# Turning gate rows on TensorE instead of by DMA, one result bank, and a new written-out order, in a fused dynamic-convolution and top-1 expert kernel

## The chip, the cores and the metric

One core of a Trainium2 chip runs the whole kernel. The metric is the device time of one execution in microseconds; lower is better. Engines are named as the profile names them: PE (TensorE matmuls), PEld (its weight loads), DVE (VectorE), ACT (ScalarE), POOL (GpSimd) and SP (SyncE, which here only issues transfers).

## The reference

There are 8 x 3584 = 28,672 tokens of 192 channels. The first half is a causal convolution whose 7 weights per token and head are a softmax; the second half sends every token to the one of 8 experts that its gate prefers.

```
w = softmax(weight_gen, axis=-1)                       # (8, 3584, 8 heads, 7 taps)
attn[b,s,h,:] = sum_k w[b,s,h,k] * x_pad[b, s+k, h, :]  # 24 channels a head
x = attn.reshape(28672, 192)
logits = x @ w_gate + modality_bias[modality_id]        # 8 experts
e = argmax(logits); p = softmax(logits)[e]
out[n] = p[n] * (relu(x[n] @ w1[e]) @ w2[e])            # 192 -> 1024 -> 192
```

## The kernel before

The tokens go through in 16 units of 1,792 tokens (128 partitions x 14 tokens), and each unit passes these steps; the name in brackets is the token of the step in the order string, followed by the unit's number.

- Load of weights, inputs and modality (LU, lines 366 to 379, on SP's queue).
- Softmax (A, X, SM, SN, B, and from unit 6 on BN: line 563 writes the normalised weights of half a unit into a PSUM bank instead of over the loaded ones).
- The 7 taps. In early units products (M, L581) are summed by PE (S, L593); later DVE multiplies (PQ, L569) and adds (PA, PM, L614, L618), and some sums are made by POOL's accumulating transfers (DA, L609).
- A scale for the unit from two ACT passes over the input, whose output is thrown away into a scratch tile "junk" (SA, L502).
- Rows: the sum split into a high and a low half-precision part in a row buffer (H on ACT, L624; L on DVE, L632 and L633).
- Gate: the rows of 128 tokens have to be turned so that channels lie on partitions. Units 0 to 4 do it on PE: six transposes into the single PSUM bank "gt" (T, L642), a copy to "xg" by ACT (E, L646). Units 5 to 15 do it by 14 transposing transfers on SP's queue each (XT, L653), from the row buffer straight into "xg", which has three buffers of two tokens each. Then PE multiplies (G, L666, into "lg").
- Routing (RA, RB and others on DVE), a table of the next expert batches (TB on DVE, read by SP), and 14 scatters of the rows to DRAM by POOL (SC, L738).

The experts' half works on 138 batches ("pages" in the code) of 128 or 256 rows of one expert: 51 of 128 and 87 of 256. A batch is fetched by a transposing transfer (PL, L960, into "xT", four buffers) and its expert's weights, if they changed, by another (PW, L979, 1.8 MB). PE computes the first layer in groups of 1,024 PSUM columns (HM, L1002, 225 groups, two buffers of two banks), ACT takes relu to "hi" (HA, L1014), DVE the remainder "lo" (HL, L1018), PE the second layer (OM, 24 matmuls at L1029 to L1031, 225 groups, into "g2", two banks), ACT scales the result into "ot" (OA, L1036) and POOL scatters it (OS, L1041).

PSUM has eight banks: four for the first layer, two for the second, and one each for "gt" and "lg". The softmax weights of BN share the bank of "gt", which in those units has no transposes.

Nothing is scheduled at run time: every engine takes its instructions in the order of the string ORDER, one token a step, and the instructions wait on semaphores for what they read and overwrite. The string interleaves the batches of earlier units with the convolution of later ones.

Of the kernel before, what the change touches and what calls it, by code (L numbers as in the profile page):

```python
# [63 lines left out]
T.0.3 S.1.0.2 wlo.3.0 E.0.3 wld.6 wpf.2 wpf.3 wlo.3.1 G.0.3 wsq.5.0 T.0.4 E.0.4 wst.2 M.1.0.3 T.0.5 wst.3 wsq.5.1 G.0.4
M.1.0.4 S.1.0.3 E.0.5 M.1.0.5 XB.2 G.0.5 T.0.6 M.1.0.6 S.1.0.4 E.0.6 A.2 G.0.6 wtr.5 S.1.0.5 RA.0.0 X.2 wmx.5 wts.2
RA.0.1 BP.2 RA.0.2 wsc.5 M.1.1.0 XM.2 S.1.0.6 wts.3 RA.0.3 wsq.6.0 wdg.5 M.1.1.1 RX.0 RA.0.4 SA.2.0 wbc.5 M.1.1.2
S.1.1.0 RA.0.5 SM.2 wsf.5 H.1.0 RA.0.6 S.1.1.1 M.1.1.3 whi.4.0 wld.7 RB.0.0 L.1.0 wsq.6.1 RR.0 S.1.1.2 whi.4.1 RB.0.1
wlo.4.0 SE.0 SN.2 wpf.4 T.1.0 SA.2.1 RB.0.2 S.1.1.3 wlo.4.1 whi.5.0 RB.0.3 wst.4 M.1.1.4 wts.4 E.1.0 RB.0.4 S.1.1.4
# [1073 lines left out]
```

## Time and profile before

| | |
|---|---|
| three timed runs, median (lowest to highest) | 1264.75 us (1251.67 to 1268.13) |
| the profiled execution, its own time | 1245.94 us |
| its span, first to last instruction | 1244.2 us |
| mean granted TensorE clock | 0.955 of full |
| PE busy | 1118.4 us (90%) |
| DVE busy | 969.5 us (78%) |
| ACT busy | 581.3 us (47%) |
| POOL busy | 651.7 us (52%) |

The span falls into three stages. Up to about 150 us no expert batch has begun. From there to about 1008 us, where the last gate matmul ends, PE works on batches while DVE works on the convolution. After that only batches are left. A busy share of PE is modelled for pipelined matmuls, so the count of instructions in a stretch of time tells more than its busy time.

### The profile page before, as it was taken

The page shows a single profiled execution, that of the slowest core. Times are in us where ns is not written, and L with a number is a line of the kernel's source. Part 1 is how long each engine was busy: PE and PEld are TensorE (multiplying, and loading weights), DVE is VectorE, ACT ScalarE, POOL GpSimd, SP SyncE. Part 2 cuts the span into 40 slices and gives each one's busy share as a digit, 9 for nine tenths or more (in the row PEclk, how much of TensorE's full clock was granted, in tenths as well). Part 3 has the DMA queues.
Part 4 walks back from the last instruction along what each step waited for, and adds up shares of the span by engine and source line. Part 5 has one row for each costly group of instructions (what it writes and reads, how often), then busy time and mean ns, then how long its engine had stood idle before and what let it go on. Part 6 is the DMA issues. An engine that isn't in the chain of part 4 may idle for free.

```text
span 1244.2 us, 31134 instructions
## 1 busy us (share of the span) xinstructions
PE 1118.4 (90%) x12304; PEld 1007.8 (81%) x12304; DVE 969.5 (78%) x1197; ACT 581.3 (47%) x1025; POOL 651.7 (52%) x561
## 2 busy tenths in 40 slices
PE   6698897599799799999799969997979999999997
PEld 3344497599689799999699959997969999999997
DVE  7799999699789799999599969999788852322231
ACT  3987274374445345464345434544333433333432
POOL 5007778488745566666337663657365465222222
PEclk9799998899989899999799989999999999999999
DMA  9988779987888778889989897969698644142243
GB/s 312 311 309 328 239 161 277 136 178 174 208 192 172 147 192 167 186 173 242 177 175 167 187 222 142 223 128 181 132 188 178 119 119 97 43 136 72 50 134 118
DMA packets 241110, 220.55 MB, mean 177 GB/s; under 512 B 198593, under 2 KB 215229, under 8 KB 235586
## 3 DMA queue, kind: packets, MB, share of 16 engines
q1 hardware_dynamic: 211776, 137.75, 45.4%
q0 software_dynamic: 29184, 80.77, 31.6%
q8 instruction: 98, 1.61, 0.6%
q14 instruction: 52, 0.42, 0.1%
HBM read 305.03 MB, written 60.05 MB: 293 GB/s over the span
## 4 chain that ended last, share of the span: by engine, by line
PE 58%; DMA 17%; issue 9%; DVE 6%; SPq 3%; POOL 3%; ACT 2%; POOLq 0%; DVEq 0%; ACTq 0%
PE g L1002 30%; PE g L1029 9%; PE g L1031 9%; PE g L1030 9%; DMA xg<-rows 6%; DMA xT<-rows_scratch 5%; POOL out_dram L1041 2%; DMA rows_scratch<-rows,idx 2%; DVE prod L581 2%; DMA wc<-in_moe_w_dram 2%; SPq L653 1%; DMA w<-weights_scratch 1%; PE lg L666 1%; PE acc L593 1%; DMA xt<-in_x_dram 1%
## 5 line engine op out<-in xcount | busy, mean ns | idle before, releaser
L1002 PE MATMUL g<-xT,w 128*128 128x256 f16 (+1 forms) x5520 | 548.9, 258 | 15.5 <-DMA xT<-rows_scratch 14.4
L1002 PEld LDWEIGHTS <-w 128*128 128x128 f16 x5520 | 464.8, 100 | 58.4 <-issue 11.0
L1031 PE MATMUL g<-w,lo 128*128 128x192 f16 x1800 | 446.8, 248 | 14.9 <-DVE lo L1018 13.9
L1041 POOL DMA_INDIRECT out_dram<-ot,meta x225 | 257.1, 1143 | 366.7 <-ACT ot L1036 311.9
L1029 PE MATMUL g<-w,hi 128*128 128x192 f16 x1800 | 446.5, 248 | 0.0
L1030 PE MATMUL g<-w,hi 128*128 128x192 f16 x1800 | 446.5, 248 | 0.0
L1018 DVE SCALAR_TENSOR_TENSOR lo<-g,hi 128x1024 f16<-128x1024 f32 x225 | 273.3, 1215 | 217.7 <-ACT hi L1014 217.0
L738 POOL DMA_INDIRECT rows_scratch<-rows,idx x224 | 327.3, 1461 | 156.1 <-ACT rows L733 78.6
L1014 ACT ACTIVATE hi<-g 128x1024 f16<-128x1024 f32 x225 | 229.9, 1022 | 349.9 <-PE g L1002 343.2
L1031 PEld LDWEIGHTS <-lo 128*128 128x128 f16 x1800 | 177.7, 99 | 18.9 <-DVE lo L1018 17.4
L1036 ACT ACTIVATE ot<-g,gm 128x192 f32<-128x192 f32 x225 | 94.0, 418 | 188.1 <-PE g L1031 117.3
L1030 PEld LDWEIGHTS <-hi 128*128 128x128 f16 x1800 | 177.7, 99 | 1.9
L1029 PEld LDWEIGHTS <-hi 128*128 128x128 f16 x1800 | 177.6, 99 | 1.9
L614 DVE TENSOR_TENSOR sum<-sum,tmp 128x1344 f32<-128x1344 f32 x78 | 120.3, 1543 | 0.0
L593 PE MATMUL acc<-prod,ident 128*128 128x512 f32 (+1 forms) x240 | 101.7, 573 | 17.9 <-DVE prod L581 17.8
L593 PEld LDWEIGHTS acc<-prod,ident 128*128 128x128 f32 x240 | 46.0, 199 | 64.2 <-issue 54.4
L569 DVE TENSOR_TENSOR tmp<-gt,xt 128x1344 f32<-128x1344 f32 x60 | 92.6, 1543 | 0.0
L609 POOL DMA_DIRECT2D sum<-prod x53 | 51.5, 979 | 49.4 <-DMA sum<-prod 16.2
L666 PE MATMUL lg<-wg,xg 128*128 128x16 f16 x672 | 34.3, 171 | 47.2 <-DMA xg<-rows 45.1
L666 PEld LDWEIGHTS <-xg 128*128 128x128 f16 x672 | 31.6, 98 | 52.3 <-DMA xg<-rows 47.4
L581 DVE TENSOR_TENSOR prod<-xt,wt 128x1344 f32<-128x1344 f32 x41 | 63.0, 1550 | 4.4 <-PE acc L593 4.3
L569 DVE TENSOR_TENSOR prod<-gt,xt 128x1344 f32<-128x1344 f32 x40 | 61.7, 1543 | 0.0
(138 smaller groups left out, 825.4 us busy)
## 6 DMA issues: line engine op xcount, KB each, us to landing
w<-weights_scratch SPq DMA_DIRECT2D x138, 1792.5 KB
sum<-prod POOLq DMA_DIRECT2D x53, 672.0 KB
xt<-in_x_dram SPq DMA_DIRECT2D x15, 1920.0 KB
weights_scratch<-hw SPq DMA_DIRECT2D x8, 1280.5 KB
wt<-in_weight_gen_dram SPq DMA_DIRECT2D x16, 392.0 KB
wc<-in_moe_w_dram SPq DMA_DIRECT2D x8, 768.0 KB
wa<-in_moe_w_dram SPq DMA_DIRECT2D x8, 512.0 KB
weights_scratch<-hw SPq DMA_DIRECT2D x16, 256.0 KB
```

The costliest lines, as they stand in the source:

```text
L569: return nc.vector.tensor_tensor(to.rearrange("p t (h g) -> p t h g", h=H), win, xin, ALU.mult)
L593: nc.tensor.matmul(un[u]["psum", c][:, q], lhsT=ident32, rhs=un[u]["pr", c, k][:, q], start=(k == order[0]), stop=(k == order[-1]))
L614: return nc.vector.tensor_tensor(a, a, un[u]["tmp"], ALU.add)
L738: i = nc.gpsimd.indirect_dma_start(out=rows, out_offset=bass.IndirectOffsetOnAxis(ap=idx[:, j:j + 1], axis=0), in_=ri[:, j, 0:ROW // 2], i ...
L1002: nc.tensor.matmul(o, lhsT=wt[:, w0:w0 + P], rhs=xT[:, xi, :pt], start=(q * pt % 512 == 0 and j == 0), stop=(j == 4), skip_group_check=True)
L1014: return nc.scalar.activation(hi, pg["ps", grp], AF.Relu)
L1018: return nc.vector.scalar_tensor_tensor(lo, live[i]["ps", grp], 0.0, hi, op0=ALU.max, op1=ALU.subtract)
L1029: nc.tensor.matmul(ps, lhsT=hi, rhs=wt[:, w0:w0 + D], start=(f == 0), stop=False)
L1030: nc.tensor.matmul(ps, lhsT=hi, rhs=wt[:, w0 + D:w0 + 2 * D], start=False, stop=False)
L1031: nc.tensor.matmul(ps, lhsT=lo, rhs=wt[:, w0:w0 + D], start=False, stop=(f == NFT - 1))
L1036: nc.scalar.activation(ot, pg["out", t], AF.Copy, scale=pg["gm"][:, t:t + 1])
L1041: w = nc.gpsimd.indirect_dma_start(out=out, out_offset=bass.IndirectOffsetOnAxis(ap=pg["meta"][:, t, 1:2], axis=0), in_=pg["res", t], in_o ...
```

## The change

Five edits:

1. Units 5 to 15 turn their gate rows on PE as units 0 to 4 did: the 88 XT steps (154 transposing transfers) go, 77 T steps and 77 E steps come. G is then done in seven steps of two tokens in these units too, with the same 42 matmuls a unit. "xg" gets four buffers.
2. The second layer's results get one PSUM bank instead of two. The bank that comes free holds the softmax weights, so "gt" is free for transposes.
3. BN, softmax weights in PSUM, begins at unit 4 instead of unit 6.
4. The scratch tile that takes the thrown-away output of the scale passes has one-byte elements instead of two-byte ones.
5. The order string is made anew, as far as the end of the last batches of the middle stage; the tail differs in a few places.

A step that loads a unit's input in pieces (LX) is added too, but no token of the new order uses it.

```
-XG = 3
-PS1 = 2
+XG = 4
+XCUTS = (0, 5, 10, 15, 20)
+PS1, PS2 = 2, 1
...
-HM.37.0 OA.36.1 ... XT.7.3 TB.6.0 PQ.7.1.6 OS.36.0 G.7.1 ...
+T.7.0 OA.35.1 PW.39 HM.37.0 E.7.0 HL.36.1 ... T.7.1 HA.37.0 OM.36.0 ... E.7.1 GM.37 T.7.2 ...
...
-        junk = att.tile([P, half * D], BF16, name="junk", bufs=1)
+        junk = att.tile([P, half * D], U8, name="junk", bufs=1)
...
-            pool["wn"] = psg.tile([P, 512], F32, name="gt")
+            pool["wn"] = (pool["psw"] if PS2 == 1 else psg).tile([P, 512], F32, name="wn" if PS2 == 1 else "gt")
...
-            junk = att.tile([P, (HALO + TU) // 2 * D], BF16, name="junk", bufs=1)
+            junk = att.tile([P, (HALO + TU) // 2 * D], U8, name="junk", bufs=1)
...
-        if fn == "HM" and args == [0, 0]:
+        if (fn == "BN" and PS2 == 1 or name == "HM.0.0") and "ps1" not in pool:
             early_ps.close()
             pool["ps1"] = ctx.enter_context(tc.tile_pool(name="ps1", bufs=PS1, space=PSUM))
-            pool["ps2"] = ctx.enter_context(tc.tile_pool(name="ps2", bufs=2, space=PSUM))
+            pool["ps2"] = ctx.enter_context(tc.tile_pool(name="ps2", bufs=PS2, space=PSUM))
+            if PS2 == 1:
+                pool["psw"] = ctx.enter_context(tc.tile_pool(name="psw", bufs=1, space=PSUM))
```

(The two lines of the order are cut from longer ones.)

What moves on SP's queue is shown at the load of unit 13: "xt" is that load, "xT" and "meta" a batch, "w" an expert's weights, "xg" gate rows of unit 11 being turned, and TENSOR_LOAD reads the table of batches. Before:

```order
L377 DMA xt<-in_x_dram 128x3840
L379 DMA mt<-in_moe_modality_id_dram 128x28
L947 TENSOR_LOAD tb
L960 ISA
L960 DMA_TRANSPOSE xT<-rows_scratch 128x3x256
L962 ISA
L962 DMA meta<-rows_scratch 128x2x2
L653 DMA_TRANSPOSE xg<-rows_73 128x3x128 x2
L979 ISA
L979 DMA w_1076<-weights_scratch 128x3585
```

And now, from the same load on:

```order
L382 DMA xt<-in_x_dram 128x3840
L384 DMA mt<-in_moe_modality_id_dram 128x28
L959 TENSOR_LOAD tb
L972 ISA
L972 DMA_TRANSPOSE xT<-rows_scratch 128x3x256
L974 ISA
L974 DMA meta<-rows_scratch 128x2x2
L991 ISA
L991 DMA w_1115<-weights_scratch 128x3585
L959 TENSOR_LOAD tb
L972 ISA
```

The transposes of gate rows behind the load are gone, and the next batch's transfers follow directly.

What moves on ACT is shown where unit 11's first rows are turned: "hi" and "ot" are the two evictions of a batch, "gm" its scale, "se", "sm" and "rows_72" small steps of the units' softmax and routing. Before:

```order
L730 ACTIVATE se<-se 128x14
L1036 ACTIVATE ot<-g_10615,gm 128x192
L1014 ACTIVATE hi<-g_10653 128x1024
L531 ACTIVATE wt<-wt 128x784
L1036 ACTIVATE ot<-g_10695,gm 128x192
L542 ACTIVATE sm<-sm 128x112
L733 ACTIVATE rows_72<-se,sf 128x14
L1014 ACTIVATE hi<-g_10736 128x1024
```

And now:

```order
L742 ACTIVATE se<-se 128x14
L999 ACTIVATE gm<-meta,w_1114 128x2
L1048 ACTIVATE ot<-g_10752,gm 128x192
L658 ACTIVATE xg<-gt 128x768
L1026 ACTIVATE hi<-g_10791 128x1024
L658 ACTIVATE xg<-gt 128x768
L1048 ACTIVATE ot<-g_10841,gm 128x192
L745 ACTIVATE rows_72<-se,sf 128x14
L658 ACTIVATE xg<-gt 128x768
L1026 ACTIVATE hi<-g_10884 128x1024
```

Three copies of turned rows now stand between the evictions, one about every half batch.

## Rows read from the trace of the kernel before

**Rows 1.** Page, part 4: the chain that ended last, by line.
```profile
PE g L1002 30%; PE g L1029 9%; PE g L1031 9%; PE g L1030 9%; DMA xg<-rows 6%; DMA xT<-rows_scratch 5%; POOL out_dram L1041 2%; DMA rows_scratch<-rows,idx 2%; DVE prod L581 2%; DMA wc<-in_moe_w_dram 2%; SPq L653 1%; DMA w<-weights_scratch 1%; PE lg L666 1%; PE acc L593 1%; DMA xt<-in_x_dram 1%
```

**Rows 2.** Stretches of 40 us: PE, PEld, DVE, ACT, POOL, clock, DMA, GB/s.
```profile
320.00:360.00 40.00, 33.84 (x312) 29.57 (x311) 31.89 (x37) 18.39 (x33) 26.25 (x22) 0.87 0.99 240
...
400.00:440.00 40.00, 32.32 (x337) 29.37 (x335) 30.57 (x42) 16.60 (x30) 22.30 (x19) 0.91 0.74 147
440.00:480.00 40.00, 40.00 (x458) 37.87 (x457) 39.75 (x53) 21.52 (x42) 28.78 (x22) 1.00 0.85 191
...
600.00:640.00 40.00, 35.04 (x328) 31.74 (x329) 33.27 (x34) 12.89 (x21) 15.17 (x14) 0.83 0.91 173
...
720.00:760.00 40.00, 29.84 (x308) 27.07 (x306) 27.93 (x33) 15.31 (x31) 19.60 (x20) 0.87 1.09 201
...
840.00:880.00 40.00, 32.04 (x336) 29.79 (x334) 30.37 (x40) 16.77 (x31) 27.51 (x23) 0.87 0.99 196
...
920.00:960.00 40.00, 31.13 (x318) 28.24 (x317) 28.86 (x32) 11.74 (x19) 23.24 (x20) 0.87 0.89 172
```

**Rows 3.** Waits over the whole span: in total us, times, longest.
```profile
ACT ot L1036 <- PE g L1031: 117.3, 95, 9.2
...
PE lg L666 <- DMA xg<-rows: 45.1, 13, 10.0
ACT rows L624 <- DVE sum L618: 24.1, 10, 11.3
...
PE g L1002 <- DMA xT<-rows_scratch: 14.4, 4, 7.0
...
PE gt L642 <- ACT xg L646: 8.7, 6, 2.7
```

**Rows 4.** Chain of waits, 718 to 746 us: start, length, what.
```profile
719.53 0.08 PE g L1031
719.62 2.18 PE g L1002 x20
...
724.43 18.04 DMA xg<-rows
```

**Rows 5.** SP's queue as a timeline, 717 to 731 us: start, length, what it issued.
```profile
717.12 0.37 SPq L377 DMA_DIRECT2D xt<-in_x_dram  x1
...
721.20 7.50 SPq L653 DMA_TRANSPOSE xg<-rows  x2
```

**Rows 6.** L1002 alone in two of the stretches, columns PE, PEld, clock, DMA, GB/s.
```profile
440.00:480.00 40.00, 22.19 (x190) 18.07 (x188) 1.00 0.85 191
...
720.00:760.00 40.00, 17.77 (x137) 13.87 (x134) 0.87 1.09 201
```

**Rows 7.** L1029 alone in the same two stretches.
```profile
440.00:480.00 40.00, 17.99 (x74) 7.23 (x74) 1.00 0.85 191
...
720.00:760.00 40.00, 12.24 (x50) 4.91 (x51) 0.87 1.09 201
```

**Rows 8.** Waits of the stretch 600 to 640 us alone.
```profile
PE g L1031 <- DVE lo L1018: 4.7, 1, 4.7
```

**Rows 9.** Chain of waits, 255 to 262 us, around two groups of transposes.
```profile
257.88 0.35 PE gt L642 x6
258.23 2.23 PE g L1002 x40
```

**Rows 10.** Groups by line and shape: busy, mean ns, idle before and its releaser.
```profile
L502 ACT ACTIVATE junk<-xt 128x1920 bf16<-128x1920 f32 x32 | 57.5, 1795 | 7.0 <-DMA xt<-in_x_dram 6.9
...
L646 ACT ACTIVATE xg<-gt 128x768 f16<-128x768 f16 x35 | 28.0, 801 | 15.2 <-PE gt L642 15.1
...
L642 PE MATMUL gt<-ident,rows 128*128 128x128 f16 x210 | 19.8, 229 | 19.9 <-ACT xg L646 8.7 <-ACT rows L624 4.8 <-DVE rows L632 4.0
```

**Rows 11.** The tail, 1160 to 1166 us, as a timeline of ACT and PE.
```profile
1161.31 2.40 PE L1002 MATMUL g<-xT,w 128*128 128x128 f16 x40
...
1161.56 0.42 ACT L1036 ACTIVATE ot<-g,gm 128x192 f32<-128x192 f32 x1 [0.82 <-ACT gm L987]
```

More of the change, by code (lines that the diff above doesn't have):

```diff
@@ L13 @@
 I32 = mybir.dt.int32
+U8 = mybir.dt.uint8
 AF = mybir.ActivationFunctionType
@@ L64 @@
[L64 to L68, printed above, removed]
@@ new lines @@
+RA.0.3 wsc.5 A.2 RX.0 wld.7 RA.0.4 X.2 wdg.5 M.1.1.3 wbc.5 wsq.6.0 RA.0.5 S.1.1.3 M.1.1.4 wsf.5 whi.4.0 RA.0.6 SM.2
+wsq.6.1 RR.0 RB.0.0 wlo.4.0 T.1.0 S.1.1.4 whi.4.1 RB.0.1 M.1.1.5 whi.5.0 RB.0.2 S.1.1.5 wlo.4.1 SE.0 E.1.0 whi.5.1
+RB.0.3 wlo.5.0 T.1.1 wsq.7.0 RB.0.4 wlo.5.1 GW.0 E.1.1 SC.0.0 SN.2 T.1.2 wsq.7.1 RB.0.5 B.2 G.1.0 G.1.1 E.1.2 SC.0.1
+TB.0.0 M.1.1.6 wpf.4 wpf.5 wtr.7 wst.4 wst.5 G.1.2 wts.4 SC.0.2 TB.0.1 S.1.1.6 wmx.7 TB.0.2 wsc.7 M.2.0.0 SC.0.3 wts.5
+TB.0.3 wdg.7 TB.0.4 M.2.0.1 wbc.7 H.1.1 S.2.0.0 SC.0.4 TB.0.5 M.2.0.2 wsf.7 RI.1 whi.6.0 SC.0.5 S.2.0.1 TB.0.6 L.1.1
@@ new lines @@
+PL.21 TB.3.9 BP.6 OS.16.0 OM.17.0 TB.3.10 PQ.5.0.4 HA.18.0 E.4.3 SC.3.7 HL.18.0 PL.22 HM.19.0 TE.4 OA.17.0 GM.18 SA.6.0
+OS.17.0 TB.3.11 PA.5.0.4 PW.21 G.4.3 SC.3.8 TB.3.12 T.4.4 PQ.5.0.2 HA.19.0 OM.18.0 E.4.4 PL.23 SC.3.9 HL.19.0 GM.19
+SA.6.1 G.4.4 T.4.5 DA.5.0.2 TB.3.13 PQ.5.0.5 HM.20.0 PW.22 E.4.5 SC.3.10 A.6 OA.18.0 SB.6 G.4.5 OS.18.0 T.4.6 OM.19.0
+HA.20.0 PA.5.0.5 E.4.6 SC.3.11 X.6 HM.21.0 HL.20.0 PW.23 SI.6 OA.19.0 PQ.5.0.6 GM.20 SC.3.12 G.4.6 OM.20.0 HA.21.0
+OS.19.0 RA.4.0 PA.5.0.6 GM.21 SC.3.13 HM.21.1 HL.21.0 OA.20.0 PW.24 RA.4.1 OS.20.0 BN.5.1 RA.4.2 PQ.5.1.0 HM.22.0
@@ new lines @@
+SE.5 HL.29.1 HM.30.0 OA.28.1 PW.32 OS.28.1 RB.5.1 PQ.6.1.4 T.6.0 HA.30.0 OM.29.0 RB.5.2 PA.6.1.4 E.6.0 GM.30 HL.30.0
+T.6.1 OA.29.0 HM.30.1 E.6.1 OS.29.0 RB.5.3 PQ.6.1.2 T.6.2 RB.5.4 HA.30.1 PL.34 OM.29.1 SM.7 DA.6.1.2 GW.5 RB.5.5
+PQ.6.1.5 E.6.2 SC.5.0 SN.7 G.6.0 OA.29.1 HM.31.0 PW.33 HL.30.1 OS.29.1 TB.5.0 B.7 SC.5.1 G.6.1 TB.5.1 G.6.2 HA.31.0
+PA.6.1.5 OM.30.0 GM.31 SC.5.2 HL.31.0 HM.31.1 OA.30.0 TB.5.2 SC.5.3 PQ.6.1.6 OS.30.0 TB.5.3 OM.30.1 PA.6.1.6 LU.8
+HA.31.1 SC.5.4 PL.35 HL.31.1 HM.32.0 OA.30.1 TB.5.4 SC.5.5 BN.7.0 TB.5.5 PW.34 TB.5.6 PQ.7.0.0 OS.30.1 OM.31.0 HA.32.0
@@ new lines @@
+PQ.8.0.4 T.7.3 HA.40.0 OM.39.0 SC.6.7 TB.6.11 E.7.3 PA.8.0.4 TE.7 GM.40 SA.9.1 G.7.3 SC.6.8 T.7.4 HL.40.0 HM.40.1
+TB.6.12 PQ.8.0.2 SC.6.9 E.7.4 OA.39.0 SB.9 G.7.4 T.7.5 PL.44 OS.39.0 TB.6.13 PQ.8.0.5 OM.39.1 HA.40.1 DA.8.0.2 E.7.5 A.9
+HM.41.0 SI.9 PW.43 OA.39.1 SC.6.10 HL.40.1 X.9 G.7.5 T.7.6 HA.41.0 PA.8.0.5 OS.39.1 OM.40.0 E.7.6 HL.41.0 GM.41 G.7.6
+OA.40.0 HM.41.1 PQ.8.0.6 SC.6.11 OS.40.0 RA.7.0 PA.8.0.6 OM.40.1 HA.41.1 SC.6.12 RA.7.1 HL.41.1 HM.42.0 OA.40.1 PW.44
+SC.6.13 RA.7.2 BN.8.1 RA.7.3 PQ.8.1.0 RX.7 OS.40.1 OM.41.0 HA.42.0 RA.7.4 PQ.8.1.1 GM.42 HM.42.1 OA.41.0 HL.42.0
@@ new lines @@
+SC.9.0 OM.56.1 HA.57.1 PL.61 TB.9.0 B.11 HL.57.1 SC.9.1 G.10.1 OA.56.1 G.10.2 PW.60 HM.58.0 TB.9.1 PA.10.1.5 OS.56.1
+TB.9.2 PQ.10.1.6 OM.57.0 HA.58.0 SC.9.2 TB.9.3 GM.58 PA.10.1.6 LU.12 HM.58.1 OA.57.0 SC.9.3 HL.58.0 TB.9.4 OS.57.0
+BN.11.0 OM.57.1 HA.58.1 TB.9.5 PL.62 TB.9.6 PQ.11.0.0 SC.9.4 HM.59.0 HL.58.1 OA.57.1 PW.61 OS.57.1 TB.9.7 PM.10.1
+OM.58.0 SC.9.5 HA.59.0 TB.9.8 PQ.11.0.1 H.10.1 HM.59.1 SC.9.6 HL.59.0 OA.58.0 XB.12 GM.59 RI.10 DA.11.0.1 TB.9.9 L.10.1
+TE.10 OM.58.1 HA.59.1 PL.63 OS.58.0 TB.9.10 PQ.11.0.3 T.10.3 OA.58.1 PW.62 HM.60.0 SC.9.7 E.10.3 HL.59.1 XM.12 OS.58.1
@@ new lines @@
+OA.61.0 HL.62.0 OS.61.0 RA.10.5 PM.11.0 DA.11.1.1 OM.61.1 HA.62.1 PL.66 HL.62.1 H.11.0 HM.63.0 RA.10.6 PQ.11.1.3 PW.65
+OA.61.1 OS.61.1 RB.10.0 RR.10 L.11.0 HA.63.0 OM.62.0 SE.10 GM.63 HL.63.0 T.11.0 OA.62.0 RB.10.1 HM.63.1 PQ.11.1.4 E.11.0
+OS.62.0 RB.10.2 PA.11.1.4 T.11.1 HA.63.1 PL.67 OM.62.1 E.11.1 RB.10.3 HL.63.1 T.11.2 RB.10.4 OA.62.1 PW.66 PQ.11.1.2
+HM.64.0 GW.10 E.11.2 OS.62.1 RB.10.5 SM.12 DA.11.1.2 G.11.0 OM.63.0 TB.10.0 HA.64.0 PQ.11.1.5 SC.10.0 SN.12 GM.64
+HL.64.0 G.11.1 SC.10.1 OA.63.0 G.11.2 HM.64.1 TB.10.1 B.12 OS.63.0 TB.10.2 PA.11.1.5 OM.63.1 HA.64.1 PL.68 SC.10.2
@@ new lines @@
+RA.11.5 L.12.0 HM.70.0 OA.68.1 PW.72 HL.69.1 OS.68.1 RA.11.6 PQ.12.1.4 RR.11 HA.70.0 T.12.0 OM.69.0 RB.11.0 GM.70
+PA.12.1.4 E.12.0 SE.11 HL.70.0 T.12.1 OA.69.0 HM.70.1 E.12.1 OS.69.0 RB.11.1 PQ.12.1.2 T.12.2 RB.11.2 HA.70.1 SM.13
+PL.74 OM.69.1 DA.12.1.2 E.12.2 RB.11.3 HL.70.1 SN.13 HM.71.0 RB.11.4 OA.69.1 PW.73 PQ.12.1.5 GW.11 OS.69.1 RB.11.5 B.13
+G.12.0 SC.11.0 OM.70.0 HA.71.0 TB.11.0 PA.12.1.5 GM.71 SC.11.1 HL.71.0 G.12.1 OA.70.0 G.12.2 HM.71.1 TB.11.1 SC.11.2
+PQ.12.1.6 OS.70.0 OM.70.1 TB.11.2 PA.12.1.6 HA.71.1 LU.14 SC.11.3 PL.75 HL.71.1 HM.72.0 OA.70.1 TB.11.3 SC.11.4 BN.13.0
@@ new lines @@
+TB.11.4 PQ.13.0.0 PW.74 OS.70.1 OM.71.0 HA.72.0 TB.11.5 PQ.13.0.1 GM.72 SC.11.5 HM.72.1 OA.71.0 HL.72.0 DA.13.0.1
+TB.11.6 PM.12.1 SC.11.6 XB.14 OM.71.1 HA.72.1 PL.76 TB.11.7 PQ.13.0.3 H.12.1 HM.73.0 PW.75 SC.11.7 OA.71.1 HL.72.1 RI.12
+OS.71.0 TB.11.8 L.12.1 OM.72.0 HA.73.0 OS.71.1 GM.73 HL.73.0 XM.14 T.12.3 HM.73.1 TB.11.9 BP.14 SC.11.8 E.12.3 TB.11.10
+PQ.13.0.4 TE.12 OA.72.0 SA.14.0 OS.72.0 TB.11.11 PA.13.0.4 G.12.3 T.12.4 PL.77 OM.72.1 SC.11.9 HA.73.1 TB.11.12
+PQ.13.0.2 E.12.4 HM.74.0 SC.11.10 PW.76 OA.72.1 HL.73.1 SA.14.1 DA.13.0.2 TB.11.13 PQ.13.0.5 G.12.4 T.12.5 HA.74.0
@@ new lines @@
+OM.73.0 SC.11.11 A.14 E.12.5 OS.72.1 GM.74 SB.14 G.12.5 T.12.6 HL.74.0 HM.74.1 X.14 E.12.6 PA.13.0.5 SC.11.12 SI.14
+OA.73.0 G.12.6 OM.73.1 HA.74.1 PL.78 SM.14 RA.12.0 SN.14 HL.74.1 SC.11.13 HM.75.0 OA.73.1 PW.77 RA.12.1 PQ.13.0.6
+OS.73.0 OS.73.1 RA.12.2 OM.74.0 PA.13.0.6 HA.75.0 GM.75 HL.75.0 HM.75.1 OA.74.0 RA.12.3 OS.74.0 BN.13.1 RX.12 RA.12.4
+PQ.13.1.0 OM.74.1 HA.75.1 PL.79 RA.12.5 PQ.13.1.1 HM.76.0 OA.74.1 PW.78 HL.75.1 OS.74.1 RA.12.6 PM.13.0 DA.13.1.1 RR.12
+HA.76.0 OM.75.0 GM.76 HL.76.0 H.13.0 RB.12.0 PQ.13.1.3 HM.76.1 SE.12 OA.75.0 OS.75.0 RB.12.1 L.13.0 OM.75.1 HA.76.1
@@ new lines @@
+PL.80 RB.12.2 HL.76.1 T.13.0 OA.75.1 PW.79 HM.77.0 RB.12.3 E.13.0 PQ.13.1.4 OS.75.1 RB.12.4 PA.13.1.4 GW.12 T.13.1
+HA.77.0 OM.76.0 SC.12.0 E.13.1 HL.77.0 GM.77 T.13.2 RB.12.5 PQ.13.1.2 OA.76.0 SC.12.1 G.13.0 E.13.2 HM.77.1 OS.76.0
+TB.12.0 PQ.13.1.5 G.13.1 DA.13.1.2 G.13.2 HA.77.1 PL.81 OM.76.1 TB.12.1 B.14 SC.12.2 HL.77.1 HM.78.0 OA.76.1 TB.12.2
+PW.80 PA.13.1.5 SC.12.3 TB.12.3 PQ.13.1.6 OM.77.0 HA.78.0 SC.12.4 GM.78 HL.78.0 LU.15 HM.78.1 OA.77.0 OS.76.1 TB.12.4
+PA.13.1.6 OS.77.0 TB.12.5 BN.14.0 OM.77.1 HA.78.1 PL.82 TB.12.6 TB.12.7 PQ.14.0.0 SC.12.5 HM.79.0 OA.77.1 PW.81 HL.78.1
@@ new lines @@
+OS.82.1 RB.13.1 PQ.14.1.2 T.14.2 RB.13.2 PQ.14.1.5 HA.84.0 DA.14.1.2 OM.83.0 E.14.2 HL.84.0 GM.84 HM.84.1 OA.83.0
+RB.13.3 B.15 OS.83.0 RB.13.4 PA.14.1.5 GW.13 OM.83.1 HA.84.1 PL.88 SC.13.0 RB.13.5 TB.13.0 PQ.14.1.6 G.14.0 OA.83.1
+HM.85.0 SC.13.1 PW.87 HL.84.1 OS.83.1 TB.13.1 PA.14.1.6 G.14.1 G.14.2 HA.85.0 OM.84.0 SC.13.2 TB.13.2 GM.85 BN.15.0
+HL.85.0 SC.13.3 HM.85.1 OA.84.0 TB.13.3 PQ.15.0.0 OS.84.0 TB.13.4 OM.84.1 PQ.15.0.1 HA.85.1 PL.89 SC.13.4 HL.85.1
+DA.15.0.1 HM.86.0 OA.84.1 PW.88 TB.13.5 PM.14.1 SC.13.5 OM.85.0 TB.13.6 PQ.15.0.3 H.14.1 SC.13.6 HA.86.0 TB.13.7 L.14.1
@@ new lines @@
+HM.86.1 OA.85.0 OS.84.1 GM.86 RI.14 HL.86.0 T.14.3 HA.86.1 PL.90 OM.85.1 TB.13.8 SC.13.7 PQ.15.0.4 E.14.3 OS.85.0
+HL.86.1 G.14.3 OA.85.1 T.14.4 PW.89 HM.87.0 E.14.4 OS.85.1 TB.13.9 PA.15.0.4 TE.14 SC.13.8 TB.13.10 PQ.15.0.2 G.14.4
+T.14.5 HA.87.0 OM.86.0 SC.13.9 E.14.5 HL.87.0 GM.87 DA.15.0.2 TB.13.11 G.14.5 PQ.15.0.5 OA.86.0 T.14.6 HM.87.1 E.14.6
+SC.13.10 TB.13.12 TB.13.13 PA.15.0.5 OS.86.0 G.14.6 OM.86.1 HA.87.1 PL.91 RA.14.0 PQ.15.0.6 SC.13.11 HM.88.0 HL.87.1
+OA.86.1 PW.90 OS.86.1 RA.14.1 PA.15.0.6 OM.87.0 HA.88.0 SC.13.12 RA.14.2 BN.15.1 GM.88 HL.88.0 HM.88.1 SC.13.13 OA.87.0
@@ L376, in load_unit @@
         else:
-            queue.dma_start(xt.rearrange("p t d -> p (t d)"), src(0, P, -HALO, n))
+            z = XCUTS[1] if f"LX.{u}.1" in tokens else n
+            queue.dma_start(xt[:, 0:z, :].rearrange("p t d -> p (t d)"), src(0, P, -HALO, z))
         m32 = mod.bitcast(I32)
@@ L381, in load_unit, with load_more @@
         un[u] = {"x": xt, "w": wt, "m": mt}
+    def load_more(u, q):
+        a, z = XCUTS[q], XCUTS[q + 1]
+        t0 = (u // 2) * S + (u % 2) * TU
+        nc.sync.dma_start(un[u]["x"][:, a:z, :].rearrange("p t d -> p (t d)"),
+                          bass.AP(tensor=x.tensor, offset=(t0 + a - HALO) * D, ap=[[TP * D, P], [1, (z - a) * D]]))
     def first_tokens(u):
```

353 lines of the change are left out of this document (150 added, 203 removed).

## The prediction

> **What bounds the kernel now.** I read the chain that ended last first. Its matmul lines L1002 and L1029 to L1031 make 57% of the span, and the largest share that is no engine's work is "DMA xg<-rows", 6% [rows 1], some 72 us: PE waits for gate rows that a transfer turns. Next I cut the middle stage into stretches of 40 us [rows 2]. They come in two sorts. In a good one (440 to 480) PE does 458 matmuls at full clock and DVE is busy for 39.75 of 40 us: both are full, so PE and DVE pace each other. In six of the 17 stretches from 320 to 1000 us (320, 400, 600, 720, 840, 920) PE does 308 to 337 matmuls, stands idle for 5 to 10 us, is granted a mean clock of 0.83 to 0.91, and DVE idles 7 to 12 us beside it. [...]
>
> The table of waits names the cause: lg waits for xg 13 times, 45.1 us in all, up to 10.0 us each [rows 3]. One of them is seen in full: at 717.12 SP issues the 1.9 MB load of a unit, then two gate transposes take 7.5 us to issue [rows 5], and the one on the chain lands 18.04 us after its issue [rows 4]. Counted in the old order, mostly three or four matmul groups (about 2.1 us each) stand between such a transfer (pieces 3 to 7 of a unit) and its gate matmul, some 8 us of cover for a landing of 18. A batch's fetch stands 11 to 13 groups ahead of its first matmul, 24 to 27 us.
>
> **Step 1, the gate waits that go.** The six bad stretches hold 1939 matmuls, 323.2 each, 134.8 fewer than the good one. At the good stretch's pace (40/458 = 0.0873 us) that is 11.8 us each, 70.6 us together. The missing ones are not all of mean cost: in the stretch at 720, L1002 misses 53 [rows 6] at 2.18/20 = 0.109 us, 5.8 us, and each second-layer line misses 24 [rows 7], three lines at 0.08 us [rows 4], 5.8 us; 11.6 us instead of 150 x 0.0873 = 13.1. So I take 0.89 of 70.6: 62.6 us. From below the term is bounded by the waits alone, 45.1 us [rows 3]; from above by idle plus clock, 240 - 194.2 = 45.8 us and 0.13 x 240 = 31 us, 77 us [rows 2], which counts time twice where PE was idle at the low clock. One piece is not the gate's: 4.7 us in the stretch at 600, where PE waited for "lo" [rows 8]. -57.9 us are left.
>
> What is late next? The batches' fetches, with cover of 26 us against that landing of 18; they cost PE 14.4 us in the whole span [rows 3]. With 154 transposes gone from SP's queue they are issued no later than now, and I book no gain for that.
>
> **Step 2, the transposes on PE.** 77 groups of six. On the chain a group takes 0.35 us, and the first-layer group behind it runs 40 matmuls in 2.23 us [rows 9]: +27.0 us, all on PE, which is the bound. The mean of 229 ns per transpose [rows 10] overlaps its neighbours; six of those would be 1.37 us.
>
> [...]
>
> The waits of a group are the uncertain part. "gt" is one bank, so a group waits for ACT's copy of the group before, 801 ns [rows 10]. In units 0 to 4 this cost 8.7 us in six cases [rows 3], and with the waits for row parts 8.7 + 4.8 + 4.0 = 17.5 us for 35 groups [rows 10], 0.5 each; for 77 that is 38.5 us. But in those units 16 of the 30 steps from one group to the next have no batch matmul between. Of the 66 new ones none is without: at least one matmul group of 2 us stands between any two, more than the copy's 0.8. And a half's first transposes stand at least one matmul group (about 2 us) behind the step that makes its last row part, but for one of 22. I take 0 of 0 to 38.5 us. G keeps its matmuls; the wait moves with the T step.
>
> **Step 3, the copies on ACT.** 77 x 0.801 = 62 us more. In the good stretch ACT is busy for 21.5 of 40 us [rows 2]; 5.6 us a unit more (a unit takes about 62 us) is 25 of 40. The cover is ACT's idle time, and if "hi" is late behind a copy, it is by 0.8 us at most. 0 us.
>
> **Step 4, one result bank.** A second-layer group may start only when the "ot" before it has been read out. In the tail the first-layer group after a result starts at 1161.31 and "ot" runs from 1161.56 for 0.42 us [rows 11]: 0.67 us after the result's end the bank is free. In the new order 214 of the 224 results have one or two first-layer groups of 2.2 us before them, which covers 0.67. Ten follow another result without one between (before it was eleven, with the second bank free): 10 x 0.67 = +6.7 us. The ends: 0, and 0.67 x 225 = 151 us if nothing covered it.
>
> [...]
>
> **Step 5, the rest.** Weights in PSUM for units 4 and 5 swap one pass for two half passes on DVE, as units 6 to 15 do, and nothing on PE; 0. One-byte scratch: no row shows a one-byte output; ACT takes 1795 ns for 1920 elements with a two-byte one [rows 10] and 801 ns for 768 of another shape, so length and not width sets it. If a pass took half or twice as long, ACT would gain or lose 29 or 57 us, nearly all under its idle time; 0. The new order has as many batches begun at unit 5's gate (28, before 27) and five more matmul groups left for the tail, which takes from the middle what it gives to the end: 0, within 8.
>
> **Sum.** 1245.9 - 57.9 + 27.0 + 6.7 = 1221.7 us for an execution like the profiled one. That one is below all three timed runs; the fastest is 5.7 us above it, the median 18.8. I keep the 5.7. The other 13 us are about as long as one of the stalls that go, and I take it for more of the same kind of waiting. 1221.7 + 5.7 = 1227.4: I say 1227, 3.0% below the median.
>
> **Rivals.** *A. The transfer waits come back elsewhere.* The unit load and the weights keep the transfers as busy as before (1.09 at 720, [rows 2]); if a fetch of a batch lands over 26 us after its issue, PE stalls there, or DVE, whose sums also come by transfer. For it: "rows" already waits 24.1 us for such sums, once 11.3 [rows 3], and DVE has no slack in the good stretch. Against it: batches waited only four times, 14.4 us. Half of the 57.9 us back: 1227 + 29 = 1256, no change that can be told.
>
> *B. The single result bank stops PE, and it is slower.* Place: ACT's queue, where "ot" now stands behind a copy that waits for PE, and behind row parts that wait for DVE. Price: 0.67 us for each result whose "ot" is not done 2.2 us after its matmuls. 167 results lie before the last gate step. It eats the gain of 38 us on the median with 56 late results, and makes the kernel slower by 2% from 63/0.67 = 94 on; with two thirds late, 112, 1227 + 75 = 1302. Against it: ACT waits for PE's results 117.3 us in 95 cases [rows 3], so it is early more often than late.
>
> *C. Transposes do not overlap* each other next to batches: 462 x 0.229 = 106 us instead of 27 [rows 10], 1227 + 79 = 1306. [rows 9] speaks against it. [...]
>
> **Chances.** Forecast 0.73: from 1202 (the upper bound of step 1 less the 4.7 us, 72, instead of 57.9, and the range of step 5) to 1239. A 0.17, B 0.07, C 0.03. A change of 2% is about what a measurement of this kernel can tell from none: 1239.5 and 1290. Faster takes nearly all of the forecast's case, 0.72; the same is A and the forecast's edge, with part of B, 0.19; slower the rest, 0.09. The range goes from 1198 to 1258, a little beyond A.
>
> **What would show it.** In the changed profile the line "lg <- DMA xg" is gone after unit 5, L654 (the transposes) has 672 matmuls paced at about 0.06 us, the stretches from 320 to 1000 us have 1.00 as clock and some 460 matmuls each, and the last gate matmul ends near 950 us with a tail of about 260. Step 1 is wrong if bad stretches remain with another name on the wait; step 2 if "gt" waits for "xg" or "rows" add up to over 10 us; step 4 if "g" of L1041 waits for "ot" more than a dozen times. The forecast as a whole is wrong if DVE, though never waiting for PE, ends the convolution no earlier than now.

## The result, and the profile after

| | before | after |
|---|---|---|
| median (lowest to highest) | 1261.55 us (1251.67 to 1268.13) | 1222.09 us (1221.76 to 1222.94) |
| profiled execution, its span | 1245.94, 1244.2 | 1221.91, 1220.1 |
| ratio, 95% interval | | 0.973 [0.968, 0.977] |

The change makes the kernel 2.7% faster; 1227 was forecast. Chips differ by more than a per cent here (the median of the kernel before was 1244.8 us on one and 1262.3 on another), so every ratio below is taken against the kernel before on the same chip; a run more than 1.5% above its kernel's fastest is left out of the ratios, but not of the medians.

Busy time and granted clock, from the page of the changed kernel:

```profile
PE 1134.3 (93%) x12766; PEld 1018.2 (83%) x12766; DVE 969.4 (79%) x1199; ACT 633.8 (52%) x1102; POOL 617.1 (51%) x561
...
PEclk9898998999999999999999999999999999999999
```

The mean clock went from 0.955 to 0.984. ACT is busy 52.5 us longer, as step 3 had it within 10 us, and POOL 34.6 us less, which the forecast did not have. The stretches that answer to [rows 2]:

```profile
320.00:360.00 40.00, 37.87 (x428) 34.88 (x426) 37.26 (x46) 23.74 (x42) 22.96 (x21) 1.00 0.77 172
...
400.00:440.00 40.00, 38.79 (x450) 36.23 (x448) 37.53 (x45) 20.80 (x39) 18.49 (x16) 1.00 0.55 124
440.00:480.00 40.00, 39.05 (x439) 36.65 (x438) 38.75 (x49) 23.29 (x42) 28.36 (x23) 1.00 0.68 151
...
600.00:640.00 40.00, 39.78 (x458) 37.28 (x455) 39.97 (x55) 21.65 (x35) 24.90 (x22) 1.00 0.85 177
...
720.00:760.00 40.00, 38.97 (x435) 35.88 (x434) 38.82 (x50) 19.02 (x33) 21.28 (x20) 1.00 0.82 178
...
840.00:880.00 40.00, 39.67 (x453) 37.34 (x450) 38.85 (x50) 18.28 (x30) 20.02 (x18) 1.00 0.67 147
...
920.00:960.00 40.00, 37.06 (x435) 34.16 (x433) 23.14 (x46) 17.32 (x30) 23.98 (x23) 1.00 0.38 87
```

All six bad stretches are gone, clock 1.00 in each. But none does quite as much other work as the good one did: there are 428 to 458 matmuls, the transposes (some 28 in 40 us) among them. SP's queue behind the load of unit 13, as [rows 5], and a group of transposes on PE, as [rows 9], from the timeline of the changed kernel (start, length, what):

```profile
687.48 0.32 SPq L382 DMA_DIRECT2D xt<-in_x_dram  x1
...
690.47 1.34 SPq L972 DMA_TRANSPOSE xT<-rows_scratch  x1
...
698.79 1.26 SPq L972 DMA_TRANSPOSE xT<-rows_scratch  x1
...
703.39 0.50 PE L654 MATMUL gt<-ident,rows 128*128 128x128 f16 x6
```

Here no transfer takes over 1.34 us to issue, and between 320 and 1000 us none takes over 2.2. The 7.50 us of [rows 5], which were two transfers of 3.18 and 4.27 us, have no successor. The waits that answer to [rows 3]:

```profile
ACT ot L1048 <- PE g L1043: 79.9, 72, 2.9
ACT rows L636 <- DVE sum L630: 14.0, 13, 2.4
...
PE g L1041 <- ACT ot L1048: 12.3, 18, 2.0
...
PE gt L654 <- ACT xg L658: 10.3, 7, 2.7
```

"lg <- DMA xg" is gone. ACT's longest wait for a sum fell from 11.3 to 2.4 us. New is PE's wait for "ot", 18 times. And the groups by line and shape that answer to [rows 10]:

```profile
L658 ACT ACTIVATE xg<-gt 128x768 f16<-128x768 f16 x112 | 90.0, 804 | 23.2 <-PE gt L654 12.2 <-issue 3.6 <-PE g L1014 3.3
L654 PE MATMUL gt<-ident,rows 128*128 128x128 f16 x672 | 58.9, 222 | 18.5 <-ACT xg L658 10.3 <-ACT rows L636 2.3 <-DVE rows L645 2.1
L514 ACT ACTIVATE junk<-xt 128x1920 uint8<-128x1920 f32 x32 | 57.4, 1795 | 1.8 <-DMA xt<-in_x_dram 1.7
```

**Where the 24 us of the two profiled executions come from.** Work on batches by stage: columns PE busy (matmuls), clock, DMA share, GB/s; first the first-layer line, then one of the three equal second-layer lines. Kernel before:

```profile
0.00:320.00 320.00, 71.69 (x965) 0.93 0.90 240
320.00:960.00 640.00, 326.06 (x2677) 0.95 0.88 180
...
0.00:320.00 320.00, 53.98 (x216) 0.93 0.90 240
320.00:960.00 640.00, 262.32 (x1055) 0.95 0.88 180
```

Kernel after:

```profile
0.00:320.00 320.00, 76.57 (x1043) 0.95 0.85 249
320.00:960.00 640.00, 324.41 (x2755) 1.00 0.71 161
...
0.00:320.00 320.00, 58.25 (x232) 0.95 0.85 249
320.00:960.00 640.00, 269.46 (x1096) 1.00 0.71 161
```

With three second-layer lines the changed kernel has done 78 + 3 x 16 = 126 more batch matmuls by 320 us, and 78 + 3 x 41 = 201 more between 320 and 960. The 327 saved in the tail make up the 24.1 us of span. So in this pair of executions 126/327 of it, some 9 us, was won before 320 us, and some 15 us after. PE's first wait for a gate transfer ends at 344 us. But the 9 us are not the new order's alone, for the execution before was a poor one there. Added up in the same way, it has 1613 batch matmuls by 320 us; the kernels of the experiments below that keep the old order have 1647 to 1697, and the changed kernel has 1739, 1695 and 1711 in its three profiles. Nor does the record say that the two executions ran on one chip: PE waits 16.4 us for "issue" after and not at all before, and in the experiments the profiles of the second chip have such waits while those of the first have at most 2.0 us (last section).

### The profile page after: what moved, and what is told of

It is laid out like the page before. It is cut to its first block, busy times and chain, and to the rows that moved or that the text cites. A ratio compares the mean times of both kernels' runs of the same rounds, so it can differ in the third digit from the quotient of the medians.

```text
span 1220.1 us, 31937 instructions
## 1 busy us (share of the span) xinstructions
PE 1134.3 (93%) x12766; PEld 1018.2 (83%) x12766; DVE 969.4 (79%) x1199; ACT 633.8 (52%) x1102; POOL 617.1 (51%) x561
## 5 line engine op out<-in xcount | busy, mean ns | idle before, releaser
L1014 PE MATMUL g<-xT,w 128*128 128x256 f16 (+1 forms) x5520 | 535.9, 254 | 4.4 <-issue 1.7
L1014 PEld LDWEIGHTS <-w 128*128 128x128 f16 x5520 | 455.4, 98 | 44.1 <-issue 5.7
L1053 POOL DMA_INDIRECT out_dram<-ot,meta x225 | 264.8, 1177 | 401.0 <-ACT ot L1048 331.4
L1041 PE MATMUL g<-w,hi 128*128 128x192 f16 x1800 | 443.8, 247 | 17.2 <-ACT ot L1048 12.3
L750 POOL DMA_INDIRECT rows_scratch<-rows,idx x224 | 284.8, 1271 | 148.8 <-ACT rows L745 70.6
L581 DVE TENSOR_TENSOR tmp<-wn,xt 128x1344 f32<-128x1344 f32 x72 | 110.9, 1541 | 0.0
L658 ACT ACTIVATE xg<-gt 128x768 f16<-128x768 f16 x112 | 90.0, 804 | 23.2 <-PE gt L654 12.2
L654 PE MATMUL gt<-ident,rows 128*128 128x128 f16 x672 | 58.9, 222 | 18.5 <-ACT xg L658 10.3
L581 DVE TENSOR_TENSOR sum<-wn,xt 128x1344 f32<-128x1344 f32 x48 | 74.1, 1544 | 0.0
L581 DVE TENSOR_TENSOR prod<-wn,xt 128x1344 f32<-128x1344 f32 x48 | 74.1, 1544 | 0.0
```

Of the source, the lines that this page charges most:

```text
L581: return nc.vector.tensor_tensor(to.rearrange("p t (h g) -> p t h g", h=H), win, xin, ALU.mult)
L750: i = nc.gpsimd.indirect_dma_start(out=rows, out_offset=bass.IndirectOffsetOnAxis(ap=idx[:, j:j + 1], axis=0), in_=ri[:, j, 0:ROW // 2], i ...
L1014: nc.tensor.matmul(o, lhsT=wt[:, w0:w0 + P], rhs=xT[:, xi, :pt], start=(q * pt % 512 == 0 and j == 0), stop=(j == 4), skip_group_check=True)
L1041: nc.tensor.matmul(ps, lhsT=hi, rhs=wt[:, w0:w0 + D], start=(f == 0), stop=False)
L1053: w = nc.gpsimd.indirect_dma_start(out=out, out_offset=bass.IndirectOffsetOnAxis(ap=pg["meta"][:, t, 1:2], axis=0), in_=pg["res", t], in_o ...
```

## The experiments

Three groups of four kernels ran, the first on one chip, the other two on another. The medians of before were 1244.8, 1262.3 and 1265.7 us.

**What the gate's waits cost.** In the kernel before, pieces 3 to 7 of a unit are still transferred, but into a tile that nobody reads: the gates of tokens 6 to 13 of each partition's 14 are computed from the turned rows of earlier tokens.

```
-        xg = un[u]["xg", h] = att.tile([P, 6 * P], F16, name="xg", bufs=XG)
+        if h < 3:
+            xg = un[u]["xg", h] = att.tile([P, 6 * P], F16, name="xg", bufs=XG)
+        else:
+            xg = pool["mo"].tile([P, 6 * P], F16, name="xl", bufs=2)
+            un[u]["xg", h] = un[u]["xg", h % 3]
```

(The scratch has one-byte elements here, to make room.)

> The kernel before, with every transfer kept, but the gate matmuls of pieces 3 to 7 of units 5 to 15 read pieces 0 to 2 again (so tokens 6 to 13 of each partition go to the experts of other tokens). Theory (PE lost some 58 us to late gate pieces): 1261 - 58 = about 1203, 1192 to 1218, no lg wait for xg over 2 us and granted clock 1.00 from 320 to 1000 us. Rival (the old order and the transfer load cost the time, the wait is only where it shows): 1245 or more, with other waits in the six bad stretches.

Measured: 1212.99 us (1199.62 to 1220.58), ratio 0.969 [0.959, 0.979], about 39 us by the ratio and 32 by the medians. PE's waits, and two stretches as in [rows 2], from an execution of 1220.14 us, the second slowest of the four:

```profile
PE g L1011 <- DMA w<-weights_scratch: 18.8, 6, 8.0
PE g L1040 <- DVE lo L1027: 17.8, 15, 4.3
...
PE g L1011 <- DVE lo L1027: 11.8, 3, 7.1
```

```profile
440.00:480.00 40.00, 36.24 (x376) 33.32 (x374) 32.89 (x40) 19.74 (x35) 21.79 (x21) 0.91 0.81 184
...
720.00:760.00 40.00, 40.00 (x453) 37.95 (x451) 39.97 (x46) 21.43 (x40) 24.27 (x20) 1.00 0.93 205
```

The wait for "xg" costs the time: no such wait is over 0.8 us here, and by the ratio the kernel is faster by two thirds of the 57.9 us. But the other sign, a clock of 1.00 from 320 to 1000 us, did not come. The stretch at 720 is good now, while four others (440, 600, 640, 800) have a clock of 0.91 and 348 to 376 matmuls. The transfers are still in the queues, and in this execution PE waits 18.8 us for weights (before 0.8) and 29.6 us for "lo" (before 13.9). So the rival on record, that the load of transfers costs time whichever wait it shows in, isn't refuted for the rest.

**The turn on PE in the old order.** The kernel before with T and E steps instead of transfers, one batch group ahead of each gate step, and one result bank.

```
-HL.22.0 XT.5.0 RB.4.0 OS.21.0 PA.5.1.4 SE.4 OM.21.1 XT.5.1 HA.22.1 ...
+... GM.23 T.5.0 E.5.0 HM.23.1 OA.22.0 ... G.5.0 ...
...
-            pool["wn"] = psg.tile([P, 512], F32, name="gt")
+            pool["wn"] = pool["psw"].tile([P, 512], F32, name="wn")
...
-            pool["ps2"] = ctx.enter_context(tc.tile_pool(name="ps2", bufs=2, space=PSUM))
+            pool["ps2"] = ctx.enter_context(tc.tile_pool(name="ps2", bufs=1, space=PSUM))
+            pool["psw"] = ctx.enter_context(tc.tile_pool(name="psw", bufs=1, space=PSUM))
```

> The turn on PE and the single result bank in the old order: T and E put one matmul group ahead of each gate step, three xg buffers, two-byte scratch, weights in PSUM from unit 6. Theory: 1261 - 58 + 27 + 7 = about 1237, 1224 to 1246; what lies above 1222 is the new order's and the fourth buffer's share. Rival (the new order made the gain): 1250 or more.

Measured on the first chip: 1205.30 us (1202.61 to 1208.29), ratio 0.971 [0.964, 0.979]. The same kernel ran again beside the changed one on the other chip:

> The turn on PE and one result bank in the old order, a second time beside the changed kernel: within 5 us of it if the new order only goes with the turn, over 5 us slower if the order gained by itself.

> The changed kernel itself, to stand on the same chip as the three beside it. By its ratio of 0.973 to the kernel before: 0.968 to 0.977. If the old order with the turn on PE (ratio 0.971) is as good, the new order is worth nothing within 5 us; if the new order has a gain of its own, this kernel is over 5 us faster than the next.

Measured there: old order 1243.88 us (1234.61 to 1244.22), ratio 0.983 [0.975, 0.991]; the changed kernel 1224.25 us (1218.91 to 1226.48), ratio 0.968 [0.961, 0.976]. By the medians, on that chip the turn and the bank alone give 18 us, and the rest of the change, the new order with it, the other 20. On the first chip the old order already got 39 us by the medians; the changed kernel wasn't run there, so what the new order adds on it stays open. The old order's waits on the second chip:

```profile
PE g L1008 <- issue: 9.4, 19, 1.1
...
PE lg L672 <- ACT xg L652: 8.2, 9, 2.3
PE g L1035 <- ACT ot L1042: 8.2, 15, 0.9
```

Its last gate matmul loads at 994.4 us, on the first chip at 963.1; that of the changed kernel beside it at 956.2. Counted in the two traces of the second chip, the changed kernel is ahead of the old order by 48 batch matmuls at 320 us, 85 at 960 and 263 at 1120. So most of the 20 us is won after 960 us, where the old order is still busy with the convolution; why its convolution ends 38 us later there isn't shown.

**One result bank alone**, in the kernel before, with the two edits to "ps2" and "wn" shown above and nothing else.

> The kernel before with one result bank alone (the softmax weights in the bank that comes free). Theory of step 4: eleven results directly behind another at 0.67 us, the rest covered by a first-layer group: 1261 + 7, 1258 to 1272. Rival B: 0.67 us or more for 94 results and more, 1290 and above.

Measured: 1242.08 us (1216.60 to 1259.70), ratio 0.986 [0.973, 0.998]. PE's waits, profiled in the slowest of its runs:

```profile
PE lg L670 <- DMA xg<-rows: 65.4, 15, 16.3
...
PE g L1033 <- ACT ot L1040: 4.9, 11, 0.6
```

Eleven waits, 0.6 us at most: in this trace the bank costs 5 us, and the old stall for "xg" swamps it. The runs spread over 43 us, so their times can't show the 7 us that were expected; the 63 us of rival B they rule out.

**The new order with the transfers.** The changed kernel, T and E of units 5 to 15 replaced by seven XT steps of two transfers each, right behind the rows they turn (four buffers, as in the change).

```
-... L.5.0 DA.5.1.1 ... T.5.0 ... E.5.0 ... T.5.1 ... E.5.1 ... G.5.0 ...
+... L.5.0 XT.5.0 XT.5.1 XT.5.2 DA.5.1.1 ... G.5.0 ...
```

> The changed kernel with its T and E steps of units 5 to 15 replaced by transposing transfers right behind the rows (seven pieces of two tokens, four buffers, cover of 2 to 12 us). Theory (the transfers are late whatever the order): PE waits for xg again, 1245 to 1300. Rival (the new order made the gain): 1222 - 27 = about 1195, up to 1215.

Measured: 1271.63 us (1262.01 to 1278.46), ratio 1.022 [1.012, 1.031]. PE's waits, and SP's queue as a timeline:

```profile
PE lg L679 <- DMA xg<-rows: 77.5, 25, 19.0
```

```profile
402.44 25.39 SPq L666 DMA_TRANSPOSE xg<-rows  x8
428.76 1.22 SPq L973 DMA_TRANSPOSE xT<-rows_scratch  x1
```

Eight transposing transfers hold SP's queue for 25.39 us, and PE waits 19.0 us in that stretch. The new order by itself doesn't make the gate's waits go; moving the work off the queue does.

**Each transpose twice** in units 5 to 15 of the changed kernel.

```
-                nc.tensor.transpose(pt[:, o:o + P], rw[:, 2 * j + q, w * P:(w + 1) * P], ident16)
+                for _ in range(2 if u >= 5 else 1):
+                    nc.tensor.transpose(pt[:, o:o + P], rw[:, 2 * j + q, w * P:(w + 1) * P], ident16)
```

> The changed kernel with each transpose of units 5 to 15 made twice into the same place: 462 transposes more on PE. Theory (0.35 us for a group of six, PE the bound): +27 us over the changed kernel, 20 to 35. Rival C (they do not overlap their neighbours, 229 ns each): +106 us. If PE has slack in the middle stage: under +12.

Measured: 1246.49 us (1244.96 to 1250.96), 22.2 us above the changed kernel beside it (1224.25). 462 more transposes, so 48 ns each, 0.29 us a group of six. A doubled group in PE's timeline:

```profile
715.34 0.83 PE L660 MATMUL gt<-ident,rows 128*128 128x128 f16 x12
```

0.83 against 0.50 us: six more take 0.33. Rival C asked for 106 us here. The clock is 1.00 in every stretch from 320 to 1000 us here too.

**Two result banks again**, in the changed kernel. It takes the weights' bank, so all softmax weights are normalised in SBUF. The third group then parted the two: weights in SBUF with one bank, and edit 3 undone alone.

```
-PS1, PS2 = 2, 1
+PS1, PS2 = 2, 2
...
-... E.3.2 SC.2.3 TB.2.3 BN.4.0 TB.2.4 ...
+... E.3.2 SC.2.3 TB.2.3 TB.2.4 ...
```

(All BN steps go in the first two; of the third only BN.4 and BN.5 go.)

> The changed kernel with two result banks, and all softmax weights normalised in place in SBUF (one pass of 975 ns a unit for two of 560). Theory: the waits of a result for the bank (12.3 us in 18 cases) go, and nothing else changes: -5 to -13 us. Rival (weights in PSUM save something besides DVE's own time): same or slower.

> The changed kernel itself, to compare the other three of this call with on the same chip. All theories: about 1222 us, 1217 to 1228, as both times before, whatever the kernel before shows on this chip.

> The changed kernel with one result bank as it is, but with the softmax weights of every unit normalised in place in SBUF (no BN step), so that the bank beside it stays unused. It parts the two things that a2_two_result_banks changed at once. Theory: the weights' place in PSUM is what shortens POOL's indirect transfers (1212 against 1833 ns each between 320 and 920 us in those runs), and a second result bank is worth 5 to 10 us, so this kernel is the slowest of both: the control plus 8 to 16 us, with POOL busy near 790 us. Rival: the second bank is worth nothing and the whole difference of 4 us came from the weights: the control plus 2 to 6 us, POOL near 790 us. A second rival: POOL's longer transfers came from the second bank (more results in flight), not from the weights: control plus or minus 3 us, POOL near 620 us.

> The changed kernel with edit 3 undone alone: units 4 and 5 normalise their softmax weights in SBUF again, units 6 to 15 in PSUM. Prediction's step 5 costed this edit at nothing: control plus or minus 3 us. Theory after a2_two_result_banks: POOL's transfers are longer by about 600 ns while units 4 and 5 run (some 50 of them), so POOL is busy some 30 us longer, 640 to 650 us, but POOL has idle time there: control plus 0 to 5 us.

Measured: two banks 1228.23 us (1226.86 to 1232.67) beside the changed kernel's 1224.25; weights in SBUF with one bank 1231.91 (1228.41 to 1232.69) and edit 3 undone 1224.04 (1223.08 to 1225.35) beside 1226.27 (1222.72 to 1227.21). The two-bank kernel had been expected 5 to 13 us faster than the changed one and is 4.0 slower. So the second bank is worth 5.6 - 4.0 = 1.6 us, less than these runs spread; my 5 to 10 was wrong. Weights in SBUF cost 5.6 us; for units 4 and 5 alone they cost nothing that can be measured.

What the weights' place changes is POOL. Its scatters of rows between 320 and 920 us (busy, count) in the changed kernel, with two banks, and with one bank and weights in SBUF:

```profile
320.00:920.00 600.00, 164.68 (x136) 1.00 0.75 167
```

```profile
320.00:920.00 600.00, 247.45 (x135) 0.99 0.68 165
```

```profile
320.00:920.00 600.00, 243.43 (x136) 1.00 0.70 167
```

1211, 1833 and 1790 ns each: longer with the weights in SBUF, whatever the banks. How that can reach PE is seen in the run with edit 3 undone, where units 4 and 5 run so (timeline of POOL, DVE, ACT):

```profile
278.37 1.56 POOL L755 DMA_INDIRECT rows_scratch<-rows,idx  x1 [0.30 <-issue]
279.94 0.98 POOL L626 DMA_DIRECT2D sum<-prod  x1
...
288.75 1.56 DVE L635 TENSOR_TENSOR sum<-sum,sum 128x1344 f32<-128x1344 f32 x1 [8.26 <-DMA sum<-prod]
...
290.34 1.42 ACT L641 ACTIVATE rows<-sum,sf 128x1344 f16<-128x1344 f32 x1 [8.73 <-issue]
291.66 0.40 ACT L1053 ACTIVATE ot<-g,gm 128x192 f32<-128x192 f32 x1
```

POOL, with no gap but its 0.30 us of issue, comes late to the accumulating transfer (279.94 us; in the changed kernel beside it 270.86); DVE stands 8.26 us for it, ACT's "rows" for DVE, and "ot" behind "rows" keeps PE waiting 7.8 us, the longest wait for "ot" in that run. This run ended no later all the same, so one such stall was made good; how isn't shown.

**Three buffers for turned rows** in the changed kernel (`XG = 3`).

> The changed kernel with three buffers for turned gate rows instead of four. Theory: the gate matmuls follow a copy within a few batch groups, so three buffers are enough: control plus or minus 3 us. Rival: ACT's copy has to wait for the gate matmuls of three pairs earlier and holds up hi and ot behind it: control plus 5 to 20 us, with xg waiting for lg in the table of waits.

Measured: 1223.10 us (1222.45 to 1231.46), 3 us below the changed kernel beside it. The fourth buffer does nothing that these runs can show.

## Why the prediction was right

The forecast, 1227, is 5 us off the median of 1222.09. The sum for the profiled execution, 1221.7, even met its successor's 1221.91. Both are partly luck. On the second chip, where the old order with the turn ran beside the changed kernel, steps 1, 2 and 4 (-24.2 in the sum) gave 18 us by the medians, and the rest of the change, step 5 (0 in the sum), gave 20. The forecast's 38 us below the median came from the 24.2 and from 13 taken for more of the same waiting; the total is right there because a gain that the forecast didn't have, 20, is as large as what it had too much, 6 in the sum and the 13.

- **Step 1, the gate waits that go, -57.9.** The cause was right: "lg <- DMA xg" is gone, and the bad stretches with it. The size was too large. Between 320 and 960 us the change won 201 batch matmuls, at step 1's own price of 0.0873 us 17.5 us, after it had paid for 444 transposes at 48 ns, 21.3 us. So by the two profiles step 1 gave 17.5 + 21.3 = 39 us, or 43 with the 4.2 us that PE waits for "ot" between 320 and 920 us put to step 4. Two other ways give as much: the run with the late pieces unread 39 us, and the old order with the turn on the second chip 18 us net, 40 with the 22 that the transposes cost. The step took for granted that a bad stretch becomes as good as the one at 440, with 458 matmuls; the stretches after have 444 on average (7096 in 640 us). That nothing else is late next holds once the transfers are gone: with the transfers only unread, weights and "lo" came in their place.
- **Step 2, +27.0.** 0.35 us a group was forecast, 0.29 measured, 22 us. One transpose lasts 222 ns here, but one more in a row adds only about a fifth of that, 48 ns. The waits stayed near nothing: "gt" for "xg" 10.3 us in seven cases instead of 8.7 in six. The limit that I had set for this (10 us with "rows") is passed only because units 0 to 4 are in it; between 320 and 960 us PE has no such wait.
- **Step 3, 0.** 77 more copies, 62.0 us. ACT had the room; the gate matmuls and their weight loads wait for a copy 10.4 us in 18 cases, before 4.3 us in four.
- **Step 4, +6.7 for ten results.** 12.3 us in 18 cases stand in the trace, more than a dozen, so by the test I had set the count was wrong. Yet a second bank gave back only 1.6 us: with two banks PE waited 12.7 and 7.5 us for "lo" on its two lines, where the run with one bank and the same weights has 22.0 us for "ot". The prediction's upper end of 151 us, for a read-out that nothing covers, is far off: first-layer groups stand between the results. (Before the last gate step the new order has 164 results, not the 167 of rival B; nothing hangs on it.)
- **Step 5, 0.** This step failed in part. The one-byte output takes 1795 ns, as the two-byte one did: 0 holds. Weights in PSUM from unit 4: 0 holds too, but not for the reason given; they relieve POOL (a scatter takes 1211 ns, and 1790 with all weights in SBUF). The new order was worth more than nothing: together with edit 3 and the fourth buffer, which showed nothing when they were undone alone, and the scratch tile, it is the 20 us on the second chip, where 0 within 8 was forecast. Less of it lies before 320 us than the profiled pair suggests. PE's wait for a batch's fetch, 14.4 us [rows 3], nearly vanished there:

```profile
L1014 PE MATMUL g<-xT,w 128*128 128x128 f16 x2040 | 124.4, 221 | 3.2 <-DMA xT<-rows_scratch 1.5 <-issue 0.9 <-DMA w<-weights_scratch 0.8
```

  I had written "I book no gain for that". But the old order with the turn has 9.8 us of this wait in the whole span on the first chip and 5.3 on the second, so part of the 14.4 was that one execution's.
- **The step from the profiled execution to the median** (5.7 us kept, 13 taken for more of the same waiting) held as a number: the kernel before spread over 16 us, the changed one over 1.2. That the 13 us were such waiting isn't shown; on the second chip the turn and the bank alone gave no more than the 24.2 of the sum.
- **Rivals.** A (waits come back elsewhere) showed itself with the transfers left in the queues, not in the changed kernel. B and C fell by experiment.
- **What would show it.** Last gate matmul near 950, tail about 260: it loads at 951.6, and the tail is 268 us. Some 460 matmuls in every stretch to 1000 us did not come: up to 960 us there are 428 to 466, and in the last 40 us 358 at a clock of 0.96.

## What to carry to other kernels

A small transfer behind a large one can be late by the queue (one landed 18.04 us after its issue, [rows 4]), and turning on an engine that seems full can be cheaper: 462 transposes cost PE 22 us and gave back nearly twice that. When stalls are removed, count what the freed stretch still holds: the best stretch of the old profile was too high a mean for the new one. A part of a change that is booked at nothing wants a run of its own: here it gave half of the gain on one chip. A tile's place (SBUF or PSUM) can matter to an engine that never touches it: POOL's scatters took 1211 ns with the weights in PSUM and 1790 in SBUF.
